# New orders of the attention cycles of a three-stage kernel on Trainium2: scores, transposes, products with v and conversion steps at other places

## The chip, the cores and the metric

The kernel runs on one core of one Trainium2 chip. The metric is the device time of one execution in microseconds (us); shown for the kernel before are three timed runs and one profiled execution.

## The reference

Attention with a mask by clusters, then two feed-forward layers. Sizes: 2 batches, 8 heads, 768 positions, head size 64, 16 clusters; 1536 tokens, model width 512, hidden width 2048. The weights come as float64.

```python
q_assign = np.argmax(einsum('bhsd,hcd->bhsc', q_n, c_n), -1)   # nearest centroid of a query
k_assign = np.argmax(einsum('bhsd,hcd->bhsc', k_n, c_n), -1)
mask = q_assign[:, :, :, None] == k_assign[:, :, None, :]
scores = np.where(mask, scale * q @ k.T, -1e9)
attn = softmax(scores)
x = (attn @ v)  as (tokens, heads * head size)
h = x @ w_in;  x = (h * cos(h)) @ w_out
h = x @ w2_in; g = 0 (h<=-1), (h+1)**2/4 (between), h (h>=1);  out = g @ w2_out
```

## The kernel before

*Halves.* The attention runs first, over eight **pairs** of heads (the two heads of a pair lie side by side in the 128 partitions); then come the two layers, over blocks of 512 tokens, in fp32r matmuls with operands split in a high and a low part (`xh`, `xl`, `w`). Each engine, and the DMA queue SP with it, runs its own instructions in the order in which the program emits them, and waits for others by semaphores. So the place where a step is emitted fixes its place on all the engines that it uses.

*A cycle.* `run_cycle` (line 800) emits one cycle per pair, cycles 0 to 7, from a string of words; `BEGIN` is the string of cycle 0, `CYCLE` (and `FIRST`, the same) of cycles 1 to 5, `LATE` of 6, `LAST` of 7 (lines 884 to 888). A word is a letter, a number, and a `'` for the pair before; the letters Q, D, C, m, t, n, O, H, J stand for the pair two ahead (with `'` one ahead), L for three ahead. In the trace the first score tile of cycles 0 to 7 starts at 14.68, 41.09, 66.74, 93.72, 119.35, 144.92, 170.55 and 196.14 us.

*The words, by what they put on which engine:*

- **S**n: four score matmuls (lines 635, 638) into one of two PSUM buffers, and the row maximum `nm` on DVE (line 645); 12 tiles a pair, 0 to 5 the first head, 6 to 11 the second. **E**n: the exponential on ACT (line 653), which frees the buffer for tile n+2.
- **G**n: three transposes of exponentials on PE and a copy on ACT (lines 696, 698). **V**n: product with v for the first head (line 703), after the G's 2n and 2n+1. **T**n: a tile of the second head turned in 32 by 32 blocks on DVE (line 741). **W**n: a quarter of the product for the second head (line 757), into all four banks `big`.
- **R**0, **R**1: inverse of the row sums of a head (line 657): a reciprocal and a small transpose on DVE, four `line` copies on POOL, one write `flat` to DRAM on SP. **B**0, **B**1: the spread of it back over partitions, `rb`, on SP (lines 682, 677). **X**: `x_rows`, the first head's product times `rb`, on DVE (line 713). **Y**: its split into `xh`, `xl` on POOL. **Z**: the second head's sums from the four banks, ACT and DVE. **z**: times `rb` and split, on POOL (lines 775, 707, 788).
- **Q**n: three transposes of q or k of a later pair, a copy on ACT, and two conversions on POOL (lines 544 to 553). **D**, **C**, **m**, **t**, **n**, **O**: its nearest centroids: dot products, transposes, maxima on DVE (m: lines 579, 580; n: lines 589, 590), a multiplication on POOL (t: line 585), and rows of one-hots (`oht`). **H**0, **H**1: five stack copies per head into the score operands `st` (line 526, SP). **J**0, **J**1: four one-hot copies per head into the same (line 526, SP). **L**: loads of q and k (line 275), **v**, **r**: loads of v (lines 291, 302), all on SP.
- **w**: a step of the conversion of a float64 weight chunk (`pump`, line 213; DVE, POOL); **I**, **A**: load and begin a chunk; **h**, **g**: a first matmul, or cosine, of the weight half.

A stack tile of a pair's second head takes the buffer of the first head's of the pair before, so H1' and J1' wait for tile 5 of the running cycle. `big` has four banks: three go round among the G's, Q's, D, C, O; the fourth collects the V's; the W's need all four, so X' comes before W0', and Z' before the next G.

Of the kernel before, what the change touches and what calls it, by code (L numbers as in the profile page):

```python
# [19 lines left out]
P = 128  # L20
# [17 lines left out]
def attention_moe_moe(  # L38
# [41 lines left out]
    ident = cpool.tile([P, P], F32, name="ident")  # L80
# [147 lines left out]
    big = [ps_b.tile([P, 512], F32, name=f"big{n}") for n in range(4)]  # L228
    ring = [0, 1, 2]
# [23 lines left out]
    with ExitStack() as actx:  # L253
# [368 lines left out]
        NP = len(pairs)  # L622
# [67 lines left out]
        def p_transpose(i, g):  # L690

            kt, hf = divmod(g, 2)
            ps = bank3()
            for jj in range(HJ):
                p = ptile[NS * i + hf * HJ + jj]
                nc.tensor.transpose(ps[:, jj * P:(jj + 1) * P], p[:, kt * P:(kt + 1) * P], ident)  # L696
            pt = ap.tile([P, HS], F32, tag="pt", bufs=PT_BUFS, name=f"p{i}_t{g}")
            nc.scalar.activation(pt, ps, AF.Copy)
            pts[(i, g)] = pt

        def p_v(i, kt):
# [33 lines left out]
        def square(i, j):  # L735


            if j == 0:
                sq[i] = ap.tile([P, 24, NJ, 32], F32, tag="ptb", bufs=1, name=f"ptb{i}")
            p = ptile.pop(NS * i + NJ + j)  # L740
            nc.vector.transpose(sq[i][:, :, j], p.rearrange("p (c r) -> p c r", r=32))
# [53 lines left out]
        def scores_of(n):  # L795
            scores(n, 0)
            scores(n, 1)
            row_max(n)

        def run_cycle(c, order):  # L800


            words = order.split()
            parts = len({w.rstrip("'") for w in words if w[0] == "W"})
            for word in words:
                i = c - word.count("'")
                what, arg = word[0], int(word[1:].rstrip("'") or 0)
                if what in "QDCmtnOHJ":
                    i += 2
                elif what == "L":  # L810
                    i += 3
                elif what == "v":
                    i += 1
                if not 0 <= i < NP and what not in "wIAqhg":
                    continue
                if what == "S":
                    scores_of(NS * i + arg)
                elif what == "E":
                    row_exp(NS * i + arg)
                elif what == "T":  # L820
                    square(i, arg - NJ)
                elif what == "G":
                    p_transpose(i, arg)
                elif what == "V":
                    p_v(i, arg)
                elif what == "X":
                    x_rows(i)
                elif what == "Y":
                    x_parts(i)
                elif what == "R":  # L830
                    inverse(2 * i + arg)
                elif what == "B":
                    spread(2 * i + arg)
                elif what == "W":
                    p_v_square(i, arg, parts)
                elif what == "Z":
                    x_sum(i)
                elif what == "z":
                    x_out(i)
                elif what == "q":  # L840
                    nc.scalar.activation(spare[:, 4:5], spare[:, 3:4], AF.Sin, scale=0.0)
                elif what == "k":
                    later(2, x_out_parts, i)
                elif what == "Q":
                    if arg == 0:
                        Prep(i)
                    preps[i].turn(arg)
                elif what == "D":
                    preps[i].dots()
                elif what == "C":  # L850
                    preps[i].back()
                elif what == "m":
                    preps[i].largest()
                elif what == "t":
                    preps[i].times()
                elif what == "n":
                    preps[i].first_of()
                elif what == "O":
                    preps[i].rows()
                elif what == "H":  # L860
                    preps[i].stack(arg)
                elif what == "J":
                    preps[i].one_hots(arg)
                elif what == "L":
                    load_qk(i)
                elif what == "v":
                    load_v(i)
                elif what == "r":
                    load_vr(i)
                elif what == "I":  # L870
                    issue_chunk(arg)
                elif what == "A":
                    begin(arg)
                elif what == "g":
                    first_h(12 * (arg + 1))
                    cosine(big[h_banks[arg]], wx[0][:, NX + 2 * arg].bitcast(I32),
                           wx[0][:, NX + 2 * arg + 1])
                    begun_g.append(arg)
                elif what == "h":
                    first_h(min(ahead[0] + 1, 36))  # L880
                elif what == "w":
                    pump(arg or 1)

        BEGIN = ("m' S3 E3 G0 t' S4 G2 G4 E4 n' S5 L' E5 O' Q0 Q1 H0' S6 S7 Q2 G5 G1 E6 G3 E7 Q3 G8 H1' T6 L J0' V0 G7 S8 S9 G6 R0 E8 T7 V1 r E9 D T8 J1' G10 V2 V3 C T9 m G9 B0 G11 S10 S11 E10 t E11 n V4 ")
        FIRST = ("Q0 H0' S0 Q1 E0 S1 E1 T10' Q2 O' V5' S2 Q3 E2 T11' S3 D v' X' J0' G0 E3 S4 W0' S5 W1' J1' R1' L W2' E4 Y' E5 H1' W3' Z' S6 R0 S7 G2 G1 G3 C V0 B1' E6 m E7 T6 V1 T7 G7 G6 G5 t S8 G4 S9 G10 E8 E9 n V2 V3 r B0 G8 T8 G9 S10 G11 S11 T9 V4 E10 z' E11 ")
        CYCLE = ("Q0 H0' S0 Q1 E0 S1 E1 T10' Q2 O' V5' S2 Q3 E2 T11' S3 D v' X' J0' G0 E3 S4 W0' S5 W1' J1' R1' L W2' E4 Y' E5 H1' W3' Z' S6 R0 S7 G2 G1 G3 C V0 B1' E6 m E7 T6 V1 T7 G7 G6 G5 t S8 G4 S9 G10 E8 E9 n V2 V3 r B0 G8 T8 G9 S10 G11 S11 T9 V4 E10 z' E11 ")
        LATE = ("S0 I0 I1 E0 I2 S1 T10' E1 O' S2 T11' H0' S3 V5' E2 G0 X' S4 Y' v' E3 J0' w E4 R1' W0' w S5 E5 W1' H1' W2' A0 w R0 W3' Z' S6 S7 G1 G2 G10 E6 w w G9 V0 w G5 G3 T6 G6 S8 w B0 E7 T7 E8 J1' B1' G4 r V1 S9 G7 w E9 S10 V2 G8 w V3 E10 T8 S11 E11 G11 w z' T9 V4 ")
        LAST = ("S0 E0 w S1 T10' E1 S2 S3 V5' E2 E3 T11' X' S4 w G0 S5 v' E4 W0' W1' w W2' E5 R1' w W3' Z' S6 G3 h E6 h S7 G5 T6 G2 h E7 S8 w T7 G6 E8 Y' h B1' G1 S9 h G4 r h E9 T8 T9 z' S10 G7 V0 E10 S11 E11 R0 h q G9 T10 h h V1 G8 V2 T11 R1 h V3 h g0 w W0 W1 B1 B0 w w w w W2 G10 G11 W3 V4 h Z V5 z k X Y ")
        END = (" ")
        first_pair()  # L890
        for c in range(NP):
            run_cycle(c, {0: BEGIN, 1: FIRST, 6: LATE, 7: LAST}.get(c, CYCLE))
        run_cycle(NP, END)


# [3 lines left out]
    while len(wslot) < 2:  # L899
        n = len(wslot)  # L900
# [122 lines left out]
    for l in range(2):  # L1023
        for qi in range(NQ):
            for blk in range(NB):
                g = g_tiles(l, qi, blk)
                h = hidden(l, qi, blk, *g)
# [37 lines left out]
```

## Time and profile before

| | us |
|---|---|
| median of 3 runs (lowest, highest) | 758.57 (757.41, 761.39) |
| the profiled execution | 758.55 |
| its span, first to last instruction | 756.6 |
| PE busy | 744.2 (98%) |
| DVE, ACT, POOL busy | 593.4, 372.5, 266.8 |

Busy times are shares of the span over all stages. PE's records overlap, so busy is not peak. The windows view gives the same per stretch of time; the timeline lists one engine's instructions with the idle time before each and what ended it; SP's timeline gives the time that each DMA instruction took to issue, not to land.

### The profile page before, as it was taken

The numbers are of one execution on the slowest core, as the hardware profiler recorded it, in microseconds if no ns is written. First come the engines' busy times: TensorE is split into PE (matmuls) and PEld (weight loads), VectorE is DVE, ScalarE is ACT, GpSimd is POOL, SyncE is SP. The second block draws the span as 40 slices with busy tenths as digits, with TensorE's granted clock in tenths as the row PEclk, the third lists the DMA queues.
The fourth block names the chain that finished last, engine by engine and source line by source line (L and its number), as shares of the span: only waits on it lengthen the run. The fifth ranks groups of instructions, "written<-read, shape, count | busy, mean of one in ns | idle before, by whom it ended". The sixth has DMA issues, their size and how long they took to land.

```text
span 756.6 us, 13126 instructions
## 1 busy us (share of the span) xinstructions
PE 744.2 (98%) x4957; PEld 592.5 (78%) x4957; DVE 593.4 (78%) x961; ACT 372.5 (49%) x727; POOL 266.8 (35%) x415
## 2 busy tenths in 40 slices
PE   8899999999999999999999999999999999999998
PEld 5577777777677788888888888888888888888887
DVE  5779777978886999888688769978867886895552
ACT  5878677877775545734334443224434322322220
POOL 6454586574363365212122113422212221121110
PEclk9999999999999999999999999999999999999999
DMA  8959777977532233122022111212311221200012
GB/s 200 226 143 224 176 176 180 219 170 201 151 82 79 83 112 113 55 84 84 28 84 84 56 52 60 84 29 83 93 48 55 84 75 38 81 4 0 29 38 101
DMA packets 77710, 74.98 MB, mean 99 GB/s; under 512 B 29488, under 2 KB 69648, under 8 KB 77648
## 3 DMA queue, kind: packets, MB, share of 16 engines
q1 hardware_dynamic: 77360, 73.99, 36.5%
q8 instruction: 39, 0.64, 0.3%
q14 instruction: 23, 0.19, 0.1%
q10 hardware_dynamic: 288, 0.16, 0.1%
HBM read 50.89 MB, written 3.19 MB: 71 GB/s over the span
## 4 chain that ended last, share of the span: by engine, by line
PE 91%; DVE 4%; ACT 2%; DMA 1%; issue 1%; SPq 0%; DVEq 0%; ACTq 0%
PE y L941 11%; PE y L942 11%; PE y L943 11%; PE big L941 11%; PE big L942 11%; PE big L943 11%; PE s L635 5%; PE big L757 4%; PE s L638 4%; PE big L696 4%; PE big L703 4%; DVE nm L645 1%; PE big L544 1%; ACT p L653 1%; PE big L562 1%
## 5 line engine op out<-in xcount | busy, mean ns | idle before, releaser
L941 PE MATMUL big<-xh,w 128*128 128x512 f32 x368 | 143.4, 390 | 0.6 <-DVE g L920 0.6
L943 PE MATMUL big<-xh,w 128*128 128x512 f32 x368 | 143.2, 389 | 0.0
L942 PE MATMUL big<-xl,w 128*128 128x512 f32 x368 | 143.2, 389 | 0.0
L905 POOL TENSOR_SCALAR gh<-g 128x512 fp32r<-128x512 f32 x96 | 62.4, 650 | 196.9 <-DVE g L934 119.0
L645 DVE TENSOR_REDUCE nm<-s 128x1 f32<-128x768 f32 x96 | 90.4, 948 | 18.1 <-PE s L638 16.5
L191 POOL TENSOR_SCALAR w<-wx 128x512 fp32r<-128x512 f32 x64 | 45.2, 706 | 164.1 <-DVE wx L184 159.9
L930 ACT ACTIVATE p<-big,ones 128x512 f32<-128x512 f32 x48 | 33.2, 691 | 136.9 <-DVE m L929 136.9
L653 ACT ACTIVATE p<-s,nm 128x768 f32<-128x768 f32 x96 | 86.4, 904 | 22.2 <-DVE nm L645 19.9
L941 PEld LDWEIGHTS big<-xh,w 128*128 128x128 f32 x368 | 69.1, 188 | 15.7 <-DVE g L920 1.5
L943 PEld LDWEIGHTS big<-xh,w 128*128 128x128 f32 x368 | 69.1, 188 | 14.4
L942 PEld LDWEIGHTS big<-xl,w 128*128 128x128 f32 x368 | 69.1, 188 | 14.2
L635 PE MATMUL s<-st,st 128*128 128x384 f32 x192 | 73.8, 384 | 4.7 <-ACT p L653 3.6
L164 ACT ACTIVATE wx<-wraw 128x512 f32<-128x512 f32 x64 | 42.6, 666 | 68.5 <-DVE w L194 58.5
L941 PE MATMUL y<-gh,w 128*128 128x512 f32 x192 | 74.7, 389 | 0.0
L942 PE MATMUL y<-gl,w 128*128 128x512 f32 x192 | 74.7, 389 | 0.0
L943 PE MATMUL y<-gh,w 128*128 128x512 f32 x192 | 74.7, 389 | 0.0
L942 PE MATMUL y<-w,gh 128*128 128x512 f32 (+1 forms) x192 | 74.3, 387 | 0.0
L943 PE MATMUL y<-w,gl 128*128 128x512 f32 (+1 forms) x192 | 74.3, 387 | 0.0
L941 PE MATMUL y<-w,gh 128*128 128x512 f32 (+1 forms) x192 | 74.3, 387 | 0.0
L909 DVE TENSOR_TENSOR gl<-g,gh 128x512 fp32r<-128x512 f32 x94 | 65.1, 693 | 8.2 <-POOL gh L905 7.4
L1010 DVE TENSOR_TENSOR acc<-y,acc 128x512 f32<-128x512 f32 x71 | 48.3, 684 | 28.7 <-PE y L943 28.7
L638 PE MATMUL s<-st,st 80*128 80x384 f32 (+1 forms) x192 | 65.4, 341 | 0.0
(163 smaller groups left out, 1421.4 us busy)
## 6 DMA issues: line engine op xcount, KB each, us to landing
wraw<-in_moe_w_in_dram SPq DMA_DIRECT2D x32, 512.0 KB
wraw<-in_moe_w_out_dram SPq DMA_DIRECT2D x32, 512.0 KB, 3.5
vr<-in_v_dram SPq DMA_DIRECT2D x32, 192.0 KB, 4.6
st<-tt SPq DMA_DIRECT2D x31, 192.0 KB, 4.0
nat<-in_q_dram SPq DMA_DIRECT2D x8, 384.0 KB, 4.9
nat<-in_k_dram SPq DMA_DIRECT2D x8, 384.0 KB
st<-tt SPq DMA_DIRECT2D x8, 384.0 KB
st<-xh SPq DMA_DIRECT2D x8, 384.0 KB, 6.2
```

Source lines behind the costliest of these rows:

```text
L164: nc.scalar.activation(x, high.bitcast(F32), AF.Abs)
L191: nc.gpsimd.tensor_scalar(hi, x, 1.0, 0.0, ALU.mult, ALU.add)
L635: nc.tensor.matmul(s[:, step, :HS], qt[:, 0, cols], kt[:, 0, kc], start=True, stop=False)
L638: nc.tensor.matmul(s[:, step, :HS], qt[:rows, 1, cols], kt[:rows, 1, kc], start=False, stop=True)
L645: nc.vector.tensor_reduce(nm, s[:, :, :HS], AX.XY, ALU.max, negate=True)
L653: nc.scalar.activation(p.rearrange("p (a n) -> p a n", a=2), s[:, :, :HS], AF.Exp, bias=nm, accum_out=dens[d][:, jj:jj + 1])
L905: nc.gpsimd.tensor_scalar(hi, g, 1.0, 0.0, ALU.mult, ALU.add)
L909: side.tensor_tensor(lo, g, hi.bitcast(F32), ALU.subtract)
L941: nc.tensor.matmul(o, lh, rh, start=first, stop=False)
L942: nc.tensor.matmul(o, lh, rl, start=False, stop=False)
L943: nc.tensor.matmul(o, ll, rh, start=False, stop=last)
L1010: nc.vector.tensor_tensor(a, po, a, ALU.add)
```

## The change

All five strings are replaced by others with the same words in another order. A new letter, `i`, would emit a matmul on the identity to keep PE busy; it stands in none of the strings. Of the strings, those of cycles 1 to 5 and of cycle 6:

```diff
-                if not 0 <= i < NP and what not in "wIAqhg":
+                if not 0 <= i < NP and what not in "wIAqhgi":
...
+                elif what == "i":
+                    keep_busy(arg)
...
+        def keep_busy(n):
+            nc.tensor.matmul(big[ring[0]][:, :n * P].rearrange("p (a n) -> p a n", a=n), ident,
+                             ident.unsqueeze(1).to_broadcast([P, n, P]), start=True, stop=True)
...
-        CYCLE = ("Q0 H0' S0 Q1 E0 S1 E1 T10' Q2 O' V5' S2 Q3 E2 T11' S3 D v' X' J0' G0 E3 S4 W0' S5 W1' J1' R1' L W2' E4 Y' E5 H1' W3' Z' S6 R0 S7 G2 G1 G3 C V0 B1' E6 m E7 T6 V1 T7 G7 G6 G5 t S8 G4 S9 G10 E8 E9 n V2 V3 r B0 G8 T8 G9 S10 G11 S11 T9 V4 E10 z' E11 ")
-        LATE = ("S0 I0 I1 E0 I2 S1 T10' E1 O' S2 T11' H0' S3 V5' E2 G0 X' S4 Y' v' E3 J0' w E4 R1' W0' w S5 E5 W1' H1' W2' A0 w R0 W3' Z' S6 S7 G1 G2 G10 E6 w w G9 V0 w G5 G3 T6 G6 S8 w B0 E7 T7 E8 J1' B1' G4 r V1 S9 G7 w E9 S10 V2 G8 w V3 E10 T8 S11 E11 G11 w z' T9 V4 ")
...
+        CYCLE = ("Q0 Q1 H0' S0 Q2 E0 S1 V5' E1 v' Q3 T10' S2 T11' O' E2 S3 D X' G0 E3 L R1' J0' H1' S4 W0' S5 W1' E4 W2' W3' E5 Y' Z' S6 G1 G2 R0 J1' G3 S7 B1' C G7 E6 m T6 V0 E7 V1 t n G6 G10 G5 S8 T7 G4 S9 r E8 G8 V2 B0 T8 V3 z' E9 G11 S10 G9 S11 T9 V4 E10 E11 ")
+        LATE = ("S0 I0 I2 V5' E0 T10' S1 E1 X' S2 T11' O' I1 S3 J0' E2 G0 E3 Y' v' H0' S4 W0' w S5 W1' w W2' W3' A0 R1' E4 H1' w E5 w Z' w R0 S6 G10 G1 E6 S7 E7 r T6 G3 V0 G6 S8 T7 G2 G4 w G9 E8 S9 B0 V1 w w G5 G11 w G8 w S10 J1' V2 E9 T8 G7 S11 E10 E11 B1' V3 z' V4 T9 ")
```

In `BEGIN`, after tile 4, `G2 G4 E4 n' S5 L' E5 O' Q0 Q1 H0' S6` becomes `G0 t' n' E3 L' Q0 G4 H0' E4 Q1 S5 S6`; in `LAST`, `S1 T10' E1 S2 S3 V5' E2` becomes `S1 V5' T10' S2 w E1 S3`. `LATE` and `LAST` keep ten w's each, and `LAST` twelve h's.

*SP in cycle 4* (pair 5 is the next; `oht` rows are one-hot copies, `xh`, `xl` rows stack copies, `flat` the writes of the inverse sums, `nat` the loads of q and k, `rb` the spreads). Before:

```order
L526 DMA st1_5_0_1431<-oht5_1894 16x384 x2
L526 DMA st0_5_1_1432<-oht5_1894 16x384 x2
L526 DMA st1_5_1_1433<-oht5_1894 16x384 x2
L669 DMA flat7_2018<-line7_2013 6x128
L275 DMA nat7_0_2020<-in_q_dram 128x12x64
L275 DMA nat7_1_2021<-in_k_dram 128x12x64
L526 DMA st0_5_1_1432<-xh_73 64x2x768
L526 DMA st0_5_1_1432<-xl_74 64x768
L526 DMA st1_5_1_1433<-xh_73 64x768 x2
L526 DMA st1_5_1_1433<-xl_74 64x768
L669 DMA flat8_2110<-line8_2105 6x128
L677 DMA rb7_2140<-flat7_2018 64x768
```

Now:

```order
L275 DMA nat7_1_1938<-in_k_dram 128x12x64
L669 DMA flat7_1950<-line7_1945 6x128
L526 DMA st0_5_0_1430<-oht5_1914 16x384 x2
L526 DMA st1_5_0_1431<-oht5_1914 16x384 x2
L526 DMA st0_5_1_1432<-xh_73 64x2x768
L526 DMA st0_5_1_1432<-xl_74 64x768
L526 DMA st1_5_1_1433<-xh_73 64x768 x2
L526 DMA st1_5_1_1433<-xl_74 64x768
L669 DMA flat8_2116<-line8_2111 6x128
L526 DMA st0_5_1_1432<-oht5_1914 16x384 x2
L526 DMA st1_5_1_1433<-oht5_1914 16x384 x2
L677 DMA rb7_2135<-flat7_1950 64x768
```

The loads of `nat` move ahead of the first `flat` write, and the one-hot rows (two copies each) from ahead of it to behind it: J0' between it and the stack copies, J1' between the second write and the spread `rb7`.

*DVE in the second half of cycle 5* (`ptb` is the turning T of a tile, lines 589 and 590 are n). Before:

```order
L741 STREAM_TRANSPOSE ptb5_2554<-p66_2504 128x24x32
L741 STREAM_TRANSPOSE ptb5_2554<-p67_2523 128x24x32
L645 TENSOR_REDUCE nm68_2581<-s68_2575 128x1
L645 TENSOR_REDUCE nm69_2594<-s69_2588 128x1
L589 TENSOR_REDUCE mx7_2550<-tt6_1840 128x24
L590 TENSOR_TENSOR xh_73<-tt6_1840,mx7_2550 128x384
```

Now:

```order
L741 STREAM_TRANSPOSE ptb5_2556<-p66_2500 128x24x32
L589 TENSOR_REDUCE mx7_2553<-tt6_1840 128x24
L590 TENSOR_TENSOR xh_73<-tt6_1840,mx7_2553 128x384
L645 TENSOR_REDUCE nm68_2587<-s68_2581 128x1
L741 STREAM_TRANSPOSE ptb5_2556<-p67_2538 128x24x32
L645 TENSOR_REDUCE nm69_2601<-s69_2595 128x1
```

n stands ahead of the row maxima of tiles 8 and 9 (`nm68`, `nm69`) and no longer behind them, right after the turning of tile 6.

*DVE at the end of cycle 5 and the start of cycle 6* (`nm72` is tile 0 of pair 6, `rb10` the spread that x_rows reads, `ptb` rows T10' and T11'). Before:

```order
L645 TENSOR_REDUCE nm72_2663<-s72_2657 128x1
L645 TENSOR_REDUCE nm73_2679<-s73_2673 128x1
L741 STREAM_TRANSPOSE ptb5_2554<-p70_2633 128x24x32
L645 TENSOR_REDUCE nm74_2694<-s74_2688 128x1
L741 STREAM_TRANSPOSE ptb5_2554<-p71_2646 128x24x32
L645 TENSOR_REDUCE nm75_2708<-s75_2702 128x1
L713 TENSOR_TENSOR rb10_2614<-big3_87,rb10_2614 128x384
L645 TENSOR_REDUCE nm76_2725<-s76_2719 128x1
```

Now:

```order
L645 TENSOR_REDUCE nm72_2663<-s72_2657 128x1
L741 STREAM_TRANSPOSE ptb5_2556<-p70_2636 128x24x32
L645 TENSOR_REDUCE nm73_2680<-s73_2674 128x1
L713 TENSOR_TENSOR rb10_2616<-big3_87,rb10_2616 128x384
L645 TENSOR_REDUCE nm74_2690<-s74_2684 128x1
L741 STREAM_TRANSPOSE ptb5_2556<-p71_2649 128x24x32
L645 TENSOR_REDUCE nm75_2706<-s75_2700 128x1
L645 TENSOR_REDUCE nm76_2737<-s76_2731 128x1
```

x_rows stands behind the maxima of tiles 0 and 1 where it stood behind those of tiles 0 to 3.

## Rows read from the trace of the kernel before

**Rows 1.** The page, part 1: busy time of PE, share of the span, instructions.

```profile
PE 744.2 (98%) x4957; PEld 592.5 (78%) x4957; DVE 593.4 (78%) x961; ACT 372.5 (49%) x727; POOL 266.8 (35%) x415
```

**Rows 2.** Windows: length, busy PE, PEld, DVE, ACT, POOL, granted clock, DMA share, GB/s.

```profile
119.35:144.92 25.57, 25.57 (x329) 19.36 (x326) 20.65 (x32) 20.67 (x49) 16.06 (x26) 1.00 0.77 183
...
170.55:196.14 25.59, 24.70 (x303) 17.23 (x303) 23.01 (x36) 19.47 (x46) 10.74 (x18) 1.00 0.72 189
...
201.60:205.00 3.40, 3.40 (x13) 2.40 (x10) 2.90 (x4) 1.69 (x5) 1.51 (x1) 0.50 0.40 128
300.00:400.00 100.00, 100.00 (x443) 82.84 (x442) 82.45 (x140) 45.53 (x78) 21.67 (x33) 1.00 0.22 68
```

**Rows 3.** Timeline of PE: start, length, line, operation, [idle before, releaser]; cycles 0, 2, 7.

```profile
24.42 0.44 PE L635 MATMUL s<-st,st 128*128 128x384 f32 x1 [1.34 <-ACT p L653]
...
79.13 1.85 PE L757 MATMUL big<-ptb,vr 32*64 32x192 f32 x70 [0.90 <-issue]
...
199.20 0.44 PE L635 MATMUL s<-st,st 128*128 128x384 f32 x1 [1.05 <-ACT p L653]
```

**Rows 4.** Timeline of the SP queue in cycle 4, from the R1' write on.

```profile
132.14 0.42 SPq L669 DMA_DIRECT2D flat<-line  x1
132.61 0.68 SPq L275 DMA_DIRECT2D nat<-in_q_dram  x1
...
134.22 1.57 SPq L526 DMA_DIRECT2D st<-xh  x1
...
139.79 0.88 SPq L669 DMA_DIRECT2D flat<-line  x1
140.72 0.89 SPq L677 DMA_DIRECT2D rb<-flat  x1
...
143.78 1.29 SPq L682 DMA_DIRECT2D rb<-flat  x2
```

**Rows 5.** Timeline of POOL, cycles 4 to 6.

```profile
144.70 1.83 POOL L775 TENSOR_TENSOR xs<-xs,rb 64x768 f32<-64x768 f32 x1 [6.34 <-DMA rb<-flat]
...
156.07 1.05 POOL L666 TENSOR_SCALAR line<-turned 6x32 f32<-6x32 f32 x4 [0.31 <-DVE turned L663]
...
198.47 1.82 POOL L775 TENSOR_TENSOR xs<-xs,rb 64x768 f32<-64x768 f32 x1 [2.27 <-DMA rb<-flat]
```

**Rows 6.** Timeline of the SP queue, cycles 5 and 6.

```profile
157.66 4.40 SPq L526 DMA_DIRECT2D st<-tt  x5
...
192.53 2.48 SPq L526 DMA_DIRECT2D st<-oht  x4
195.05 0.59 SPq L677 DMA_DIRECT2D rb<-flat  x1
```

**Rows 7.** Timeline of the SP queue, cycle 1.

```profile
49.53 5.73 SPq L526 DMA_DIRECT2D st<-oht  x8
55.37 0.42 SPq L669 DMA_DIRECT2D flat<-line  x1
...
64.80 0.78 SPq L677 DMA_DIRECT2D rb<-flat  x1
```

**Rows 8.** Tile rb: landing of its transfers.

```profile
DMA to landing us min/median/max: 3.4/4.1/5.3
```

**Rows 9.** Timelines of DVE and PE at the start of cycle 6.

```profile
171.56 2.00 DVE L645 TENSOR_REDUCE nm<-s 128x1 f32<-128x768 f32 x2 [0.17 <-PE s L638]
...
177.22 0.54 DVE L713 TENSOR_TENSOR rb<-big,rb 128x384 f32<-128x384 f32 x1
...
177.62 1.38 PE L757 MATMUL big<-ptb,vr 32*64 32x192 f32 x48
```

**Rows 10.** Timelines of ACT and PE in cycle 5.

```profile
166.83 0.90 ACT L653 ACTIVATE p<-s,nm 128x768 f32<-128x768 f32 x1
...
168.56 0.42 PE L635 MATMUL s<-st,st 128*128 128x384 f32 x1
```

**Rows 11.** Groups of instructions by line and form: busy us, mean ns.

```profile
L703 PE MATMUL big<-p_t,v 128*64 128x384 f32 x192 | 39.5, 510 | 0.0
```

More of the change, by code (lines that the diff above doesn't have):

```diff
@@ L880, in run_cycle @@
                     first_h(min(ahead[0] + 1, 36))
+                elif what == "i":
+                    keep_busy(arg)
                 elif what == "w":
                     pump(arg or 1)
-        BEGIN = ("m' S3 E3 G0 t' S4 G2 G4 E4 n' S5 L' E5 O' Q0 Q1 H0' S6 S7 Q2 G5 G1 E6 G3 E7 Q3 G8 H1' T6 L J0' V0 G7 S8 S9 G6 R0 E8 T7 V1 r E9 D T8 J1' G10 V2 V3 C T9 m G9 B0 G11 S10 S11 E10 t E11 n V4 ")
-        FIRST = ("Q0 H0' S0 Q1 E0 S1 E1 T10' Q2 O' V5' S2 Q3 E2 T11' S3 D v' X' J0' G0 E3 S4 W0' S5 W1' J1' R1' L W2' E4 Y' E5 H1' W3' Z' S6 R0 S7 G2 G1 G3 C V0 B1' E6 m E7 T6 V1 T7 G7 G6 G5 t S8 G4 S9 G10 E8 E9 n V2 V3 r B0 G8 T8 G9 S10 G11 S11 T9 V4 E10 z' E11 ")
@@ L888, in attention_moe_moe @@
-        LAST = ("S0 E0 w S1 T10' E1 S2 S3 V5' E2 E3 T11' X' S4 w G0 S5 v' E4 W0' W1' w W2' E5 R1' w W3' Z' S6 G3 h E6 h S7 G5 T6 G2 h E7 S8 w T7 G6 E8 Y' h B1' G1 S9 h G4 r h E9 T8 T9 z' S10 G7 V0 E10 S11 E11 R0 h q G9 T10 h h V1 G8 V2 T11 R1 h V3 h g0 w W0 W1 B1 B0 w w w w W2 G10 G11 W3 V4 h Z V5 z k X Y ")
+        def keep_busy(n):
+            nc.tensor.matmul(big[ring[0]][:, :n * P].rearrange("p (a n) -> p a n", a=n), ident,
+                             ident.unsqueeze(1).to_broadcast([P, n, P]), start=True, stop=True)
@@ new lines, in attention_moe_moe @@
+        BEGIN = ("m' S3 G2 S4 G0 t' n' E3 L' Q0 G4 H0' E4 Q1 S5 S6 E5 O' H1' G1 E6 S7 R0 G3 Q2 V0 T6 E7 S8 G6 Q3 S9 T7 G8 J0' G5 V1 D E8 V2 B0 G7 C L m E9 S10 T8 J1' G11 T9 V3 r t G9 G10 S11 V4 E10 n E11 ")
+        FIRST = ("Q0 Q1 H0' S0 Q2 E0 S1 V5' E1 v' Q3 T10' S2 T11' O' E2 S3 D X' G0 E3 L R1' J0' H1' S4 W0' S5 W1' E4 W2' W3' E5 Y' Z' S6 G1 G2 R0 J1' G3 S7 B1' C G7 E6 m T6 V0 E7 V1 t n G6 G10 G5 S8 T7 G4 S9 r E8 G8 V2 B0 T8 V3 z' E9 G11 S10 G9 S11 T9 V4 E10 E11 ")
+        CYCLE = ("Q0 Q1 H0' S0 Q2 E0 S1 V5' E1 v' Q3 T10' S2 T11' O' E2 S3 D X' G0 E3 L R1' J0' H1' S4 W0' S5 W1' E4 W2' W3' E5 Y' Z' S6 G1 G2 R0 J1' G3 S7 B1' C G7 E6 m T6 V0 E7 V1 t n G6 G10 G5 S8 T7 G4 S9 r E8 G8 V2 B0 T8 V3 z' E9 G11 S10 G9 S11 T9 V4 E10 E11 ")
@@ new lines, in attention_moe_moe @@
+        LATE = ("S0 I0 I2 V5' E0 T10' S1 E1 X' S2 T11' O' I1 S3 J0' E2 G0 E3 Y' v' H0' S4 W0' w S5 W1' w W2' W3' A0 R1' E4 H1' w E5 w Z' w R0 S6 G10 G1 E6 S7 E7 r T6 G3 V0 G6 S8 T7 G2 G4 w G9 E8 S9 B0 V1 w w G5 G11 w G8 w S10 J1' V2 E9 T8 G7 S11 E10 E11 B1' V3 z' V4 T9 ")
+        LAST = ("S0 E0 S1 V5' T10' S2 w E1 S3 T11' E2 X' S4 E3 w R1' G0 E4 W0' v' B1' Y' w S5 W1' W2' W3' E5 w Z' w S6 G5 E6 h h S7 G3 G2 T6 S8 E7 G6 G1 h E8 T7 r S9 h h T8 G7 E9 h G4 T9 S10 h S11 V0 E10 V1 E11 w z' R0 V2 h V3 T10 q R1 G8 h h G9 T11 G10 w B0 w G11 W0 B1 h g0 W1 W2 w W3 V4 h Z w V5 X z k Y ")
```

## The prediction

> **What bounds the kernel now.** I read the page first: PE is busy for 98% of the span [rows 1]. The windows view then splits the run. In the weight half it is busy without a gap (100.00 of the 100 us after 300), a fixed amount of matrix work that the new orders do not touch. What they can move is PE's idle time in the attention half, and the same view, cut at the first score tile of each cycle, shows how little that is in the middle: cycle 4 takes 25.57 us and PE is busy for all of it [rows 2]. The losses lie at the ends. PE's timeline puts them at score tiles that wait for an exponential (1.34 us ahead of tile 5 in cycle 0, 1.05 us ahead of tile 2 in cycle 7 are the longest) and at one 0.90 us in cycle 2 that waits for nothing the profile shows [rows 3]; and from 201.6 us on, for 3.4 us, the granted clock was 0.50, that is 1.2 GHz in place of 2.4 [rows 2]. With the smaller ones I estimate some 10 us, 1.3% of the time. That is the most a reordering can win.
>
> The next view is the DMA queue's own timeline, because SP issues in program order and is nearly always issuing: in cycle 4 there is no pause from the write of the odd head's inverse sums (132.14) to the spread of the even head's (143.78) [rows 4]. The last is POOL's timeline. Once a cycle POOL sits idle until the spread of the odd head's sums has landed (6.34 us in cycle 4); then it does the product with it, splits the rows, does the four conversions of the next pair's q and k, and writes the lines of the following inverse, which SP sends off at once [rows 5]. So there is a ring that closes once per cycle: **the R1' write on SP, the issues up to B1', B1's landing, POOL's work, the next R1' write.** Before, its parts are 8.58 us (132.14 to 140.72), 3.98 us (140.72 to 144.70), and 12.42 us to the end of the next lines at 157.12, of which 0.31 us was a wait for DVE: 25.0 us in all, against a PE cycle of 25.57 [rows 2, 4, 5]. It just fits.
>
> **The change part by part.**
>
> *SP in cycles 1 to 5.* The load L moves ahead of the R1' write, and the eight small one-hot copies (J0', J1') move behind it, in between it and B1'. The transfers are the same. L took 1.61 us (132.61 to 134.22) and leaves the ring. Eight one-hot copies come in; four took 2.52 us in cycle 6 (192.53 to 195.05), so 5.04. The five stack copies took 5.57 us right behind L (134.22 to 139.79) and 4.40 in cycle 5, which has no L; with L well ahead of them I take 1.1 us off. New stretch: 8.58 - 1.61 + 5.04 - 1.1 = 10.9 us [rows 4, 6]. Bounds: 10 us if the second write, 0.93 us to the next issue, is sent as fast as the first (0.47); 12 us if the stack copies stay at 5.57 [rows 4]. The landing I take at 3.5 us, since the one B1' that stood behind four one-hot copies, as all of them now do, took 3.42 (195.05 to 198.47). POOL's part is 12.42 - 0.31 = 12.1 us, as R1' now stands ahead of a row maximum on DVE [rows 5, 6]. The ring becomes 10.9 + 3.5 + 12.1 = 26.5 us: 0.9 us longer than PE's cycle. **It slips.**
>
> *Where it bites.* In cycle 1 SP reaches the write earlier, since eight one-hot copies leave the stretch ahead of it and L enters: 55.37 - 5.84 + 1.6 = 51.1 us. Issues are slower there (55.37 to 64.80 is 9.43 us, 0.85 more than in cycle 4), so the write of cycle 2 is at 51.1 + 11.8 + 4.0 + 12.1 = 79.0 us, and three rings of 26.5 put that of cycle 5 at 158.5, where before it followed the lines that ended at 157.12 [rows 4, 5, 7]. B1' then goes out at 169.4, and the spread of the even head, B0, behind it and four v loads, 3.06 us later (140.72 to 143.78), at 172.5; its second half at 173.1. With the median landing of 4.1 us it is there at 177.2 us [rows 4, 8].
>
> *DVE at the start of cycle 6.* LATE moves x_rows (X'), which reads that spread, from behind four row maxima to behind two. Before, it ran at 177.22 and waited for nothing. Its place is now some 3.8 us into the cycle: the first maximum starts 1.0 us in (171.56 against 170.55), and two maxima of 1.0 and a transpose of 0.9 stand ahead, so 174.4 us if the cycle again starts at 170.55. The data come at 177.2, so DVE stands for 2.8 us, and tile 2's maximum stands behind it. PE runs on until tile 4, which needs the buffer of tile 2: X' to 177.7, maximum to 178.7, exponential to 179.6, tile 4 to 180.4. The products W0' start then, in place of 177.62 [rows 9]. **+2.8 us.** Bounds: 0 with a ring of 25.6, and 6 with one of 27.6.
>
> *DVE in the middle of cycles 1 to 5.* n (first_of) moves ahead of two row maxima and waits for POOL's t. What it delays is tile 9's exponential, which had ended at 167.73, where the tile that needs its buffer started at 168.56: 0.83 us of cover, about what n takes off it. I cost it at nothing; without the cover it is some 0.5 us a cycle [rows 10]. If the ring is late, t is late and PE waits there, but such a wait moves the start of cycle 6 and not the landing at 177.2, so the two are paid once.
>
> *Cycle 7.* V5' moves in between tiles 1 and 2, where PE waited 1.05 us. Its four instructions are worth 0.82 us (39.5 us over 192, times 4), which fill that [rows 3, 11]. **-0.8 us**, between 0 and -2.5 if the half-clock stretch of 3.4 us, at a loss of half of it, goes too [rows 2]. *BEGIN.* Q0, G4 and Q1 fill the 1.34 us wait ahead of tile 5, but the tiles after them then wait for exponentials that come no earlier, as the order of the maxima and of n' on DVE stays: 0, between -1.5 and +1. *The h's and w's* keep their number in each cycle, and joining or parting products with v is worth tenths: 0.
>
> Sum: 2.8 - 0.8 = +2.0 us on the profiled execution's own 758.55 us, which stands within 0.02 of the median of the three runs (758.57). **Forecast 760.5 us.** A measurement of this kernel can tell about 0.5%, 3.8 us, from no change.
>
> A rule of the Trainium skill speaks to the first part (Perfetto Trace Analysis, What "DMA-bound" means): where the issuing sequencer's track is solid, its window is descriptor generation, and what counts is the size of the descriptors. By that rule an order that keeps every transfer leaves SP's load as it was; the first rival is that case.
>
> **The rivals.**
>
> 1. *The ring does not slip* (chance 0.30). SP's issues are partly paced by transfers that back up, and not by their number, so the one-hot copies may cost less than they did alone. For it: the first stack copy took 1.57 us behind L. Against: four one-hot copies took 2.52 us even in the calm of cycle 6 [rows 4, 6]. Then X' waits for nothing, and the sum is -0.8: 757.7 us. If the 0.90 us of cycle 2, half of the 3.4 us and the good end of BEGIN (1.5) come too, 753.6 us [rows 2, 3].
> 2. *The ring slips by 2 us a cycle* (0.17): slower. It decides if the stretch on SP is 12 us in every cycle, its upper bound. Then the ring is 27.6 us, the write of cycle 5 is at 79.0 + 3 x 27.6 = 161.8 us, the spread lands 12 + 3.06 + 0.6 + 4.1 us later at 181.6, and W0' starts 7.2 us late, unless PE has paid part of that at n before: 758.55 + 7.2 - 0.8 = 765.0 us, or 762.5 where other work covers a third.
> 3. *The clock falls in cycle 6* (0.13). In cycle 7 PE stood for 1.05 us ahead of 199.20, and from 201.6 its granted clock was 0.50; all of cycle 6 was at 1.00. A stand of 2.8 us in cycle 6 is longer than that one. The price is half of 3.4 us: 760.5 + 1.7 = 762.2 us [rows 2, 3]. The Trainium skill (TensorE: Matmul & The Clock Gate, What's actually happening) says that the throttled state is the default and that activity releases it, which speaks for this rival; the trace agrees as far as cycle 7 goes.
>
> **How the numbers follow.** The forecast's own case has 0.40. Faster by over 0.5% means under 754.8 us: the better half of rival 1, 0.15. Slower means over 762.3: most of rival 2 (0.13), half of rival 3 and the edge of the forecast, 0.23 in all. The other 0.62 is no change that can be told. The likeliest case alone runs from 758 to 762 us. The range for 8 in 10 reaches from well inside rival 1, 754.5, to just short of rival 2's full price, 764.5 us.
>
> **What would show it.** The R1' write drifts by about 0.9 us a cycle against PE's first tile; POOL's product with the odd spread starts near 173 us; in cycle 6 the row of x_rows on DVE has a wait for the spread of 2 to 3 us, and tile 4 on PE one for an exponential. If the R1' writes keep 25.6 us apart, rival 1 holds; if n waits for POOL in cycles 3 to 5 by a microsecond each, rival 2; a window of PE at 0.50 near 175 to 180 us is rival 3. The forecast is wrong in kind if x_rows waits for nothing and the time still rises, or if cycle 0 changes by more than 1.5 us.

## The result, and the profile after

The changed kernel takes **767.57 us** (median of six runs, 766.77 to 771.54), the kernel before 758.35 beside it (six runs, 756.8 to 761.39): a ratio of 1.013, 95% interval 1.0096 to 1.0163. It is slower, by more than the forecast of 760.5 us allowed, and it lies above the forecast's range, which ended at 764.5. The profiled execution took 767.37 us (span 765.6, before 756.6); PE is busy for 98% of it, as it was [rows 1]:

```profile
PE 746.6 (98%) x4956; PEld 591.6 (77%) x4957; DVE 595.0 (78%) x961; ACT 372.3 (49%) x727; POOL 266.4 (35%) x415
```

The windows view of the changed kernel, cut at the first score tile of cycles 1 to 7, with one stretch of cycle 6 and the rest of the run (columns as in [rows 2]):

```profile
40.62:67.65 27.03, 26.03 (x329) 19.02 (x328) 21.23 (x33) 20.82 (x49) 12.15 (x22) 1.00 0.74 172
67.65:94.96 27.31, 26.69 (x330) 19.31 (x328) 20.72 (x32) 20.51 (x49) 16.57 (x25) 1.00 0.77 176
94.96:122.14 27.18, 26.34 (x330) 19.22 (x328) 20.79 (x32) 20.50 (x49) 16.55 (x25) 1.00 0.78 177
122.14:148.91 26.77, 26.13 (x330) 19.11 (x328) 20.68 (x32) 20.51 (x49) 16.57 (x25) 1.00 0.78 178
148.91:175.24 26.33, 25.69 (x324) 18.64 (x322) 20.34 (x31) 20.19 (x48) 16.53 (x25) 1.00 0.64 147
175.24:205.89 30.65, 26.49 (x303) 18.60 (x304) 23.05 (x37) 20.38 (x47) 14.19 (x20) 0.89 0.87 221
...
182.90:189.60 6.70, 5.03 (x57) 3.81 (x57) 3.61 (x5) 4.65 (x10) 3.38 (x5) 0.51 1.04 272
...
205.89:765.60 559.71, 553.41 (x2814) 454.60 (x2812) 439.20 (x710) 220.69 (x380) 151.80 (x207) 1.00 0.21 66
```

Cycles 1 to 5 took 134.62 us (40.62 to 175.24) where they had taken 129.46 (41.09 to 170.55): +5.2. Cycle 6 took 30.65 in place of 25.59 [rows 2]: +5.1, and in the middle of it the clock stood near 0.5 for 6.7 us. What follows cycle 6 took 559.71 us, against this row of the kernel before:

```profile
196.14:756.60 560.46, 554.71 (x2814) 455.12 (x2812) 437.67 (x710) 221.37 (x381) 151.71 (x208) 1.00 0.22 67
```

That is -0.75. The first tile of cycle 1 came 0.47 earlier. The sum, -0.5 + 5.2 + 5.1 - 0.75, is the 9.0 us by which the span grew.

*The ring.* The timeline of SP in the changed kernel (start, length, line, operation), from the R1' write of each cycle; it answers to [rows 4, 6, 7]:

```profile
52.64 1.25 SPq L669 DMA_DIRECT2D flat<-line  x1
53.98 3.40 SPq L526 DMA_DIRECT2D st<-oht  x4
...
65.72 0.59 SPq L677 DMA_DIRECT2D rb<-flat  x1
...
81.78 0.29 SPq L669 DMA_DIRECT2D flat<-line  x1
...
108.56 0.29 SPq L669 DMA_DIRECT2D flat<-line  x1
...
135.73 0.28 SPq L669 DMA_DIRECT2D flat<-line  x1
136.11 2.48 SPq L526 DMA_DIRECT2D st<-oht  x4
...
143.18 0.84 SPq L669 DMA_DIRECT2D flat<-line  x1
144.07 2.78 SPq L526 DMA_DIRECT2D st<-oht  x4
146.90 0.59 SPq L677 DMA_DIRECT2D rb<-flat  x1
...
162.55 0.29 SPq L669 DMA_DIRECT2D flat<-line  x1
```

The writes are 29.1, 26.8, 27.2 and 26.8 us apart. In cycle 4 the stretch to B1' is 146.90 - 135.73 = 11.17 us, and the one-hot copies are 5.26 of it. POOL's timeline gives the other two parts; it sat idle for some 8.7 us per cycle where it had been 6.34 in cycle 4 [rows 5]:

```profile
123.64 1.82 POOL L775 TENSOR_TENSOR xs<-xs,rb 64x768 f32<-64x768 f32 x1 [8.68 <-DMA rb<-flat]
...
150.50 1.82 POOL L775 TENSOR_TENSOR xs<-xs,rb 64x768 f32<-64x768 f32 x1 [8.78 <-DMA rb<-flat]
...
161.48 1.05 POOL L666 TENSOR_SCALAR line<-turned 6x32 f32<-6x32 f32 x4
```

B1' lands in 150.50 - 146.90 = 3.60 us; from there to the next write is 12.05. The ring is 11.17 + 3.60 + 12.05 = 26.82 us.

SP itself has time to spare in this ring. The longest of its waits in cycle 4 of the changed kernel (line, releaser, us in total, times, longest) is one that the kernel before does not have there, the R1' write waiting for POOL's lines:

```profile
SPq L669 <- POOL line L666: 3.6, 1, 3.6
...
```

Over cycles 1 to 5 there are four such waits of 16.8 us in all. So it is the time once round the ring that is too long, and not the number of issues on the queue.

*Where PE pays.* Of DVE's waits (40 to 200 us) the two of over 0.2 us that the kernel before does not have there, and the longest of PE's (40 to 240): engine, line, releaser, us in total, times, longest:

```profile
...
DVE rb L713 <- DMA rb<-flat: 3.1, 1, 3.1
DVE mx L589 <- POOL tt L585: 3.1, 5, 1.2
...
```

```profile
PE s L635 <- ACT p L653: 3.9, 7, 1.2
PE big L696 <- ACT p L653: 3.3, 1, 3.3
PE big L757 <- issue: 1.2, 3, 0.6
PE big L544 <- DMA nat<-in_k_dram: 0.8, 1, 0.8
...
```

In cycles 1 to 5 n (L589) waits for POOL's t each time, 3.1 us together; in cycles 2 and 4, where it waits for over 1 us, a score tile behind it waits for its exponential (0.4 and 0.6 us). Of the 5.2 us that these cycles lost, 2.5 are idle time of PE; the other 2.6 are in records that overlap less, and no wait in the profile accounts for them (with all one-hot copies out of the ring, below, 2.0 of them are gone). The rest of the slip is paid at once in cycle 6. DVE and PE there, against [rows 9]:

```profile
178.01 0.92 DVE L645 TENSOR_REDUCE nm<-s 128x1 f32<-128x768 f32 x1
182.07 0.56 DVE L713 TENSOR_TENSOR rb<-big,rb 128x384 f32<-128x384 f32 x1 [3.13 <-DMA rb<-flat]
```

```profile
180.88 0.38 PE L696 MATMUL big<-ident,p 128*128 128x128 f32 x2
184.57 0.48 PE L696 MATMUL big<-ident,p 128*128 128x128 f32 x1 [3.30 <-ACT p L653]
...
186.26 2.23 PE L757 MATMUL big<-ptb,vr 32*64 32x192 f32 x48
```

x_rows waits 3.13 us for its spread, PE 3.30 us behind it, and the first W0' (x48), 1.38 us long before, runs at half the clock in 2.23. Cycle 7 has these two waits at score tiles, where [rows 3] had one:

```profile
208.95 0.44 PE L635 MATMUL s<-st,st 128*128 128x384 f32 x1 [0.58 <-ACT p L653]
...
212.00 0.44 PE L635 MATMUL s<-st,st 128*128 128x384 f32 x1 [1.20 <-ACT p L653]
```

### The profile page after: what moved, and what is told of

Its sections match the earlier page's. It is cut to its first block, busy times and chain, and to the rows that moved or that the text cites. A ratio compares the mean times of both kernels' runs of the same rounds, so it can differ in the third digit from the quotient of the medians.

```text
span 765.6 us, 13116 instructions
## 1 busy us (share of the span) xinstructions
PE 746.6 (98%) x4956; PEld 591.6 (77%) x4957; DVE 595.0 (78%) x961; ACT 372.3 (49%) x727; POOL 266.4 (35%) x415
## 4 chain that ended last, share of the span: by engine, by line
PE 84%; DVE 5%; DMA 4%; ACT 3%; POOL 1%; issue 1%; SPq 1%; POOLq 0%; DVEq 0%; ACTq 0%
PE y L947 11%; PE y L948 11%; PE y L949 11%; PE big L947 11%; PE big L948 11%; PE big L949 11%; PE s L635 4%; PE big L696 3%; PE big L757 3%; PE s L638 3%; PE big L703 3%; ACT p L653 2%; DVE nm L645 2%; DMA nat<-in_k_dram 1%; PE big L544 1%
```

## The experiments

Each ratio is to the kernel before, run beside it on the same chip, with its 95% interval. Medians of kernels that were not run side by side (the changed kernel and the experiments, above all) are compared to about 1 us.

### Is it the ring?

**All one-hot copies out of the ring** (the changed kernel, cycles 1 to 5):

```diff
-... D X' G0 E3 L R1' J0' H1' S4 ... R0 J1' G3 S7 B1' C ...
+... D X' G0 E3 J0' L R1' H1' S4 ... R0 G3 S7 B1' J1' C ...
```

> The changed kernel with two moves on the SP queue in cycles 1 to 5, nothing else: J0' goes out ahead of L and R1', J1' behind B1', so that no one-hot copy lies between the R1' write and B1'. Theory 1, the ring (in the changed kernel the R1' writes are 29.1, 26.8, 27.2 and 26.8 us apart and PE is made to follow): the stretch from the write to B1' falls from 11.2 us to about 6, the writes follow PE's cycle of 25.6 to 26.0 us, x_rows in cycle 6 waits for nothing, the granted clock is 1.00 through cycle 6, and the time is 757.5 us (755.5 to 760). Theory 2, local losses (L too early, n too early, a wait at PE that has nothing to do with the ring): cycles 1 to 5 stay at 26.3 to 27.3 us and the time falls by under 2 us, to 765.5 or more.

Measured: 762.83 us (759.27 to 765.69), ratio 1.005 (1.003 to 1.0069). The writes follow 25.0, 25.2, 24.8 and 25.9 us apart; cycles 1 to 5 take 130.83 us, 3.8 less than in the changed kernel; x_rows waits for nothing, and cycle 6 is down to 25.40 us at full clock. In place of it the clock fell in cycle 7. DVE, and the windows of cycle 6 and of that fall:

```profile
175.46 0.54 DVE L713 TENSOR_TENSOR rb<-big,rb 128x384 f32<-128x384 f32 x1
```

```profile
171.85:197.25 25.40, 24.28 (x303) 17.03 (x303) 23.09 (x37) 20.22 (x47) 9.81 (x17) 1.00 0.82 210
202.90:213.50 10.60, 10.15 (x155) 7.96 (x162) 6.73 (x10) 4.51 (x11) 7.72 (x10) 0.52 0.14 38
```

So theory 1 holds in its signs but not in the time, which is 3 us above its range. The fall of the clock in cycle 7 is part of that (the two runs with a mean granted clock of 1.000 took 759.27 and 760.84 us), and so is cycle 1 with 27.09 us, which the ring does not explain.

**J1' alone out** (the second of the two moves only).

> The changed kernel with J1' alone moved out of the ring (behind B1'); J0' stays between the R1' write and the stack copies. The ring is 26.9 - 2.8 = 24.1 us, under PE's cycle. Theory 1 (only what the ring has over PE's cycle costs): the same as with all eight copies out, 762.8 us (761 to 764), and x_rows in cycle 6 waits for nothing. Theory 2 (each copy in that stretch costs, by its traffic or its place): about half of the gain, 765.2 us (764 to 766.5).

Measured: 760.79 us (757.76 to 766.82), ratio 1.0043 (1.0018 to 1.0067), just under theory 1's range and not to be told from the kernel with all eight out; x_rows ran at 175.91 without a wait. Four copies may stay in the ring for nothing, the next four cost the slip. Only what the ring has over PE's cycle is paid, as theory 1 says.

**The SP order alone, in the kernel before:**

```diff
-... D v' X' J0' G0 E3 S4 W0' S5 W1' J1' R1' L W2' ... R0 S7 ...
+... D v' X' G0 E3 S4 W0' S5 W1' L R1' J0' W2' ... R0 J1' S7 ...
```

> The kernel before with the SP order of the change and nothing else of it: in cycles 1 to 5 L ahead of the R1' write, J0' between it and the stack copies, J1' between the second write and B1'. PE, DVE, ACT and POOL keep the order of before. Theory 1: the R1' writes come 26.5 to 27.5 us apart, the spread of the even head lands near 181 us, x_rows of cycle 6 (at 177.22 before) waits for it for 3 to 4 us less what PE has paid in cycles 2 to 5, and the time is 763 us (761 to 766). Theory 2: the SP order costs nothing by itself, 758.5 us (757 to 760).

Measured: 764.58 us (764.05 to 767.38), ratio 1.0078 (1.0052 to 1.0103). The writes come 27.4, 27.2, 27.3 and 27.9 us apart. That is some 6 of the 9 us, with PE's, DVE's, ACT's and POOL's orders as before. The place where it was paid is not the one expected: x_rows waited for its spread in cycles 4 and 5 (0.44 and 1.33 us) and not in cycle 6, where PE waited 1.5 us for a late load of v.

**A longer ring with every copy where it was** (the kernel before):

```diff
-... C V0 B1' E6 ... V3 r B0 G8 ...
+... C V0 E6 ... V3 r B1' B0 G8 ...
```

> The kernel before with one move in cycles 1 to 5 and nothing of the change: B1' goes out behind the four v loads (r) in place of ahead of them; all one-hot copies and L stay where they were. The ring (R1' write, issues up to B1', landing, POOL's work) grows by those loads, some 2.1 us, from 25.0 to 27.1. Theory 1 (only the length of the ring matters): the writes come 27 us apart, x_rows waits for its spread in cycle 5 or 6, and the time is 764 us (762 to 766.5), as with the SP order of the change. Theory 2 (what costs is the copies themselves beside the products W, or their lateness): 758.5 us (757.5 to 760).

Measured: 765.45 us (763.41 to 768.2), ratio 1.0094 (1.007 to 1.0118). SP, DVE and PE in cycle 4:

```profile
147.57 0.74 SPq L669 DMA_DIRECT2D flat<-line  x1
148.41 2.30 SPq L302 DMA_DIRECT2D vr<-in_v_dram  x4
150.75 0.47 SPq L677 DMA_DIRECT2D rb<-flat  x1
```

```profile
128.86 0.56 DVE L713 TENSOR_TENSOR rb<-big,rb 128x384 f32<-128x384 f32 x1 [0.62 <-DMA rb<-flat]
...
140.10 0.21 DVE L663 STREAM_TRANSPOSE turned<-rec 128x32 f32<-128x32 f32 x1 [2.64 <-POOL line L666]
```

```profile
142.26 0.55 PE L696 MATMUL big<-ident,p 128*128 128x128 f32 x3 [2.27 <-DVE tt L580]
```

The v loads ahead of B1' take 2.30 us, and the writes are 27.6 to 28.9 us apart. x_rows waits only once in cycles 1 to 6, for 0.62 us; this kernel pays elsewhere. R0's small transpose on DVE waits for POOL's late lines of R1' (2.64 us in cycle 4), and PE stands for 2.27 us for a later step of DVE (L580), in a cycle of 30.36 us. No copy moved, and the loss is as large as that of the copies: what costs is the length of the ring, not what stands in it, and where it is paid depends on which step needs late data first.

### Where cycle 6 pays, and the clock

**x_rows back behind four row maxima** in LATE (`S1 E1 X' S2 ... E2 G0 E3` becomes `S1 E1 S2 ... E2 G0 X' E3`).

> The changed kernel with one move in LATE: x_rows (X') goes back from behind two row maxima to behind four. Theory 1: the spread lands at about 181.7 us as in the changed kernel, so x_rows still runs at about 182; but tiles 2 and 3 no longer stand behind it, PE stands for under 1 us in place of 3.3, the granted clock stays at 1.00, and W0' starts near 182.7 in place of 186.3: 762.5 us (761 to 764.5). Theory 2, that the wait only moves on to W0' and the clock falls all the same: 766 to 768 us.

Measured: 764.89 us (762.8 to 769.41), ratio 1.0091 (1.0064 to 1.0119). x_rows ran at 183.84 and waited 0.34 us; cycle 6 took 25.88 us at full clock. The range was missed by a little: in this profile, too, the clock fell in cycle 7 (0.50 from 210 to 215 us), and the runs with a mean granted clock of 1.000 took 762.8, 764.6 and 764.89. The early place of x_rows, with the fall of the clock in cycle 6, costs some 3 us on top of the ring, by medians that were not taken side by side; the ring's own slip stays, paid in cycles 1 to 5 (134.67 us).

**PE kept busy during the stand** (`J0' E2 G0` becomes `J0' E2 i4 i4 i4 i4 G0` in LATE; extra matmuls whose output is overwritten).

> The changed kernel with four matmuls on the identity (the letter i that the change brings, 512 columns each) ahead of G0 in cycle 6, where PE stands for 3.3 us behind x_rows; they write a bank that the next transposes overwrite. If the stand takes the clock down and the clock costs time of its own: the granted clock stays at 1.00 in cycle 6, PE's work from 184.6 to about 189.5 us is done in half the time, and the time is 765.0 us (764 to 766). If the matmuls are too short to fill the stand, or the clock falls for another reason, 767.5 us (766.5 to 768.5).

Measured: 765.81 us (764.51 to 767.65), ratio 1.0088 (1.0064 to 1.0112). The four fillers (eight records, 3.60 us) took most of the stand, 0.71 us of it was left, and cycle 6 is at full clock throughout:

```profile
182.49 3.60 PE L887 MATMUL big<-ident 128*128 128x512 f32 x8
185.92 0.38 PE L696 MATMUL big<-ident,p 128*128 128x128 f32 x2
187.02 0.33 PE L696 MATMUL big<-ident,p 128*128 128x128 f32 x1 [0.71 <-ACT p L653]
```

```profile
176.82:206.14 29.32, 27.73 (x313) 18.54 (x311) 23.15 (x37) 20.33 (x47) 14.23 (x20) 1.00 0.92 230
```

The mean granted clock of its four runs was 0.998 to 1.000, of the changed kernel's six 0.991 to 0.998. The fall in cycle 6 thus hangs on the stand. It is worth some 1.8 us of the 9 by the medians, which were not taken side by side; in the two profiles cycle 6 is 1.33 us shorter (29.32 against 30.65).

**The new LATE and LAST in the kernel before.**

> The kernel before with the new LATE and LAST (cycles 6 and 7) and the old BEGIN, FIRST and CYCLE. Theory 1 (the ring of cycles 1 to 5 is what makes x_rows wait in cycle 6): the R1' writes keep their 25.6 us, x_rows runs near 174.5 us and waits for nothing, PE does not stand for 3.3 us in cycle 6 and its clock stays at 1.00 there. The new LAST on its own I now take for about 1 us dearer than the old (in the changed kernel cycle 7 had waits of 0.58 and 1.20 us at score tiles and came out 0.75 us ahead only as its clock did not fall): 759 us where the clock falls for some 3 us in cycle 7, 762 where it falls for some 10 us as in the first look at the kernel with the one-hot copies out of the ring. Rival (the new place of x_rows costs by itself): a wait at x_rows of 2 us or more, 761 or more with the clock at 1.00.

Measured: 758.27 us, ratio 0.9989 (0.9974 to 1.0003). x_rows ran at 174.52 and waited for nothing: its new place costs only where the ring is late. The time is 0.7 us under the 759 expected.

**The old LAST, with the copies out of the ring.**

> The kernel with the one-hot copies out of the ring (762.83 us) with the old LAST in cycle 7. If the new LAST is what lets PE's clock fall for some 10 us there (its longest waits at score tiles were 0.57 and 1.19 us, 3 us apart): the clock falls for some 3 us at most, as in the kernel before, and the time is 759.5 us (758.5 to 760.5). If the clock falls as often with the old order, 762 to 763.5.

Measured: 760.55 us (759.25 to 762.59), ratio 1.0027 (1.0012 to 1.0043); mean clocks 0.997 to 1.000, with the new LAST 0.991 to 1.000. This is at the upper edge of what was expected for a shorter fall, and 2.3 us less than with the new LAST. But the two did not run side by side, and the kernel with J1' alone out, which has the new LAST, came to 760.79 us: a gain in time is not shown. What differs is how deep the clock falls: the lowest mean clock was 0.991 in both of the kernels with the new LAST, and 0.997 here.

**Fillers in cycle 7 of the kernel before** (`E1 S2 S3` becomes `E1 i4 S2 S3`).

> The kernel before with two filler matmuls on the identity (the word i4, 0.86 us measured ahead) ahead of tile 2 in cycle 7, where PE stood for 1.05 us before its clock fell to 0.50 for 3.4 us. If the stand takes the clock down: the clock stays at 1.00 in cycle 7 and the time falls by half of 3.4 us, to 757 us (756.3 to 757.7). If the clock falls for another reason, or PE has no such slack: 758.5 to 759.5.

Measured: 757.61 us (756.47 to 758.74), ratio 0.999 (0.9981 to 0.9999): the fastest kernel here, by a margin that its interval only just carries. The word i4 is one matmul of 512 columns, which the trace shows as two records. The start of cycle 7 up to 240 us, first of this kernel, then of the kernel before, with nearly the same instructions (the two records of the filler stand in place of two matmuls of the kernel before):

```profile
197.37:240.00 42.63, 41.62 (x545) 29.93 (x544) 33.34 (x54) 28.54 (x63) 22.10 (x30) 1.00 0.36 99
```

```profile
196.14:240.00 43.86, 41.99 (x545) 30.80 (x544) 33.06 (x54) 28.45 (x63) 22.12 (x30) 0.96 0.36 96
```

That is 1.2 us less for the stretch, at a clock of 1.00 in place of 0.96; from the start of cycle 7 to the end of the span it is 1.3 us (756.5 - 197.37 against 756.6 - 196.14). The filler saves what a fall costs and no more: the 13 runs of the kernel before beside it that had a mean clock of 1.000 have a median of 757.73 us, the 8 such runs with the filler 757.78.

**The same with the new LATE and LAST** (i2 ahead of tile 2, i4 ahead of tile 3).

> The kernel before with the new LATE and LAST (758.27 us) and filler matmuls in its two stands of cycle 7: i2 ahead of tile 2 (0.57 us there), i4 ahead of tile 3 (1.19 us). If the stands take the clock down: it stays at 1.00 and the time is 757 us (756 to 757.6), the fastest here. If not: 758 to 759.

Measured: 758.7 us, ratio 1.0008 (0.9997 to 1.0018). The clock was kept (1.00 in the profile), and the time did not fall: 1.1 us more than the kernel above, which ran beside it. That does not show the new LATE and LAST to be dearer: without fillers, their four runs with a mean clock of 1.000 had a median of 757.12 us, beside 757.23 for seven such runs of the kernel before. Part of the difference may be the fillers, of which there is one more here.

### The other parts

**The new BEGIN in the kernel before.**

> The kernel before with the new BEGIN (cycle 0) alone. Prediction's claim: 0 us, between -1.5 and +1, so 758.5 us (757 to 759.5). Rival: the new BEGIN leaves SP or DVE late for cycle 1, which was 1.4 us longer in the changed kernel and in the one with the copies out of the ring: cycle 1 takes over 26.5 us here too, and the time is 759.5 to 760.5.

Measured: 759.69 us, ratio 1.0014 (0.9999 to 1.0028). Cycle 1 took 26.15 us, 0.5 more than before and not the rival's 1.4, with PE waiting for loads of q and k (0.23 and 0.29 us). The time lies in the rival's range, the sign of it does not show: some 1 us, at the edge of what can be told, and not traced to a cause.

**n moved back, with the copies out of the ring** (`V1 t n G6` becomes `V1 t G6`, `z' E9 G11` becomes `z' E9 n G11`).

> The kernel with the one-hot copies out of the ring (762.83 us) with one more move: n goes back behind tile 9's maximum and transposed exponential in cycles 1 to 5. If n's early place costs by itself (DVE waits 0.3 us for POOL's t in cycle 5 there, PE 0.74 and 0.35 us for exponentials in cycle 1), those waits go and cycles 1 to 5 are some 1.5 to 2 us shorter together: 761 us, with the clock of cycle 7 as it falls (759 where it is at 1.00). If it costs nothing once the ring is short: 762 to 763.5, and the same cycles.

Measured: 766.3 us (761.43 to 768.9), ratio 1.0099 (1.0067 to 1.013): a miss, 3.5 us dearer. Cycles 2 to 5 took 27.4 to 27.8 us each: the second half of n (L590) now meets POOL's product or split of xs there. DVE, then POOL, in cycle 4, and the same line of the changed kernel (min, median, max in ns):

```profile
146.16 2.22 DVE L590 TENSOR_TENSOR xh<-tt,mx 128x384 fp32r<-128x384 f32 x1
```

```profile
146.14 1.83 POOL L788 TENSOR_TENSOR xl<-xs,xh 64x768 fp32r<-64x768 f32 x1
```

```profile
L590 DVE TENSOR_TENSOR xh<-tt,mx x7: 557/559/560, 24.3 to 169.2; 128x384 fp32r<-128x384 f32 x7
```

So it does not tell what n's early place costs; that stays open. With J1' alone out of the ring, n waits some 0.3 us in each of cycles 1 to 5 and no score tile waits over 0.2 us behind it. The kernel with the old LAST has one hint: in its cycle 1 (27.99 us) n waited 2.00 us for t, and a score tile 1.04 us behind it.

## Why the prediction was wrong, step by step

**The step that failed** is the size of one term, the 2.8 us by which the late x_rows was to delay W0'; it measured 8.6 us. With it failed the split of the rivals: a landing as late as rival 2's and a fall of the clock as in rival 3 came together, and the range left no room for both.

- **The ring slips** (forecast): right in kind, and nearly in size. 10.9 + 3.5 + 12.1 = 26.5 us was 11.17 + 3.60 + 12.05 = 26.82 in cycle 4.
- **Cycle 1's terms** were mis-sized. The write was put at 51.1 us and came at 52.64; the stretch behind it was put at 11.8 us and was 13.08 (four one-hot copies took 3.40 us there, not 2.52, and the write itself 1.25, not 0.42). The rows of a calm cycle were used for a crowded one. With three rings at 26.9 in place of 26.5, the write of cycle 5 was at 162.55 and not at 158.5: 4.05 us = 1.54 + 1.24 + 1.27.
- **The landing, and what X' costs.** It was put at 177.2 us, a delay of 2.8 us for W0'. x_rows ran at 182.07, 4.9 us later, and W0' at 186.26 in place of 177.62 [rows 9]: 8.6 us late, of which 4.7 had been paid by the start of cycle 6. These 8.64 us are the 2.78 forecast, 4.87 for the later landing and 0.99 of slower work between x_rows and W0', in which PE ran near half the clock; another 1.1 came between W0' and the end of cycle 6. A slip that builds up over five cycles adds up the errors of its terms: three of 1.2 to 1.5 us made 4. Rival 2 had the landing at 181.6 us and the time at 765.0, and that landing came, but not by its cause: behind cycle 1 the ring was 26.8 to 27.2 us and not 27.6, and n waited 0.30, 1.22 and 0.28 us in cycles 3 to 5 where its sign was a microsecond each.
- **"Paid once"** held in the main: with four copies out of the ring n's waits in cycles 2 to 5 fall from 2.9 us to 1.2, and the wait in cycle 6 to nothing. What is left of n's waits is not the ring's: with all eight copies out they are 2.9 us again over cycles 1 to 5, 1.7 of it in cycle 1.
- **Rival 3 came too.** Its price (1.7 us) was right to within the noise, 1.8 us in the run with the fillers. But rivals 2 and 3 were given chances as if one excluded the other, while the longer stand of the later landing is the one in which the clock fell: 765.0 + 1.7 = 766.7, within 1 us of the measured 767.57. The range ended at 764.5, short of rival 2 alone and of both.
- **Rival 1**, with the Trainium skill (Perfetto Trace Analysis, What "DMA-bound" means): by the page, the size of the descriptors is what matters where the issuing queue is solid. The trace does not bear that out for this kernel: before, the queue was solid from the R1' write to the spreads [rows 4], and the SP order alone, all transfers kept, cost 6.1 us. In the changed kernel SP stood for 16.8 us in all at the R1' write. What counted was which transfer stands behind which.
- **Cycle 7, -0.8**: -0.75 was measured, for another reason. V5' did not fill the wait; the new order has two, 0.58 and 1.20 us, in place of one of 1.05 [rows 3]. What it gained is the stretch at 0.50 [rows 2], which this profile does not have in cycle 7. That the number fits is luck: five other kernels with the new LAST had the same two waits, and in their profiles the clock did fall there, for 3 to 10 us.
- **BEGIN, 0 between -1.5 and +1**: about +1, at the upper end.
- **n ahead of two row maxima, 0**: not settled, see the last experiment.

The remaining 1.8 us of the kernel with the copies out and the old LAST are not fully explained. BEGIN alone cost about 1 us; in the profile the loss is there by the start of cycle 6 (172.45 in place of 170.55 us), with a cycle 1 of 27.99 in place of 25.65 us, and why that cycle is longer was not tested. The "issue" gaps in the products W (0.90 us once before [rows 3], 1.2 us in three places after) stay open: the profile names no releaser, and they also move between cycles in kernels that share the order of cycles 1 to 5.

## What to carry to other kernels

Where an in-order queue is nearly never idle, look for the loop that closes through it and compare its length with the cycle of the engine that bounds the kernel. Here the slack was half a microsecond: what the issues placed inside the loop took beyond it was paid in every cycle, and the same issues outside the loop cost nothing that could be told. A queue that begins to wait at an instruction of the loop, as SP did at the R1' write, was the sign here that the loop had become the longer one. A debt of that kind costs nothing until something needs the late data, so price it by the number of cycles, with the durations of the most crowded one. And where one rival's wait can set off another rival's loss, give the pair a case of its own.

## What the runs showed of the hardware that was not expected

- A DVE operation on two SBUF tensors (L590, with n moved back) took 1.90 to 2.22 us in four cycles in which a POOL operation on two tensors had begun just before it, and 0.56 us in the other three of that kernel and in all seven of the changed one; it ended 0.4 us after the POOL operation had (146.16 + 2.22 against 146.14 + 1.83). A DVE operation with one input in PSUM (L580) took 0.56 us also where it began within a POOL operation on two tensors (changed kernel, 85.25 and 139.09 us). The Trainium skill (SBUF — State Buffer, SBUF: two separate sides) has a port pair that DVE and GpSimd hold in turn for a whole instruction; the trace agrees.
- The clock fell from 1.00 to 0.50 after a wait of PE of 1.05 us (cycle 7 before) and in one of 3.30 us (cycle 6 after). The wait alone does not decide it. Seven of the kernels have the new LAST without fillers, and in cycle 7 of each PE waits twice, for 0.57 or 0.58 and for 1.18 to 1.20 us, 3 us apart. In their profiles the clock did not fall there in two (the changed kernel, and the same with fillers in cycle 6), fell for some 3 us in three and for some 10 us in two. One filler matmul of 1.02 us (two records), put into such a wait in the kernel before, went with a clock of 1.00 in the profile and mean clocks of 0.998 to 1.000 in all 11 runs; the runs of the kernel before beside it had 0.995 to 1.000.
